# Two attention blocks in one kernel: block B's output projection taken out of block A's attention loop, mask building moved ahead, score matmuls kept in fours

## The chip, the cores and the metric

The kernel runs on one core of a Trainium2 chip. The core has a matmul engine (TensorE, PE in the profile), three engines for elementwise work (VectorE or DVE, ScalarE or ACT, GpSimd or POOL), and DMA queues (here issued from SP and ACT). Matmuls write to PSUM, an accumulator memory of eight banks of 512 float32 values for each of 128 partitions; everything else lies in SBUF. The metric is the device time of one execution in microseconds (us), the median of several executions.

The kernel is written in Tile: the source gives operations on tiles, and a scheduler decides the order of instructions on each engine and adds the waits between them. A tile pool with `bufs=n` holds n tiles in rotation; a tile is given again once all that read it have finished. So the order in which TensorE runs its matmuls is not simply that of the source.

## The reference

Two independent blocks, A and B, each with x of 2048 x 640, 32 heads of 20, in bfloat16. A is attention in a sliding window of 256 positions, B is linear attention. The outputs are set side by side.

```python
def _A_ref(x, wqkv, wo):
    H = 32; Dh = D // H; W = 256
    q, k, v = ...                       # x @ wqkv, split into heads
    scores = jnp.einsum("bhqd,bhkd->bhqk", q, k) * (Dh ** -0.5)
    mask = (idx[:, None] - idx[None, :] >= 0) & (idx[:, None] - idx[None, :] < W)
    p = softmax(jnp.where(mask, scores, -1e9))
    o = jnp.einsum("bhqk,bhkd->bhqd", p, v)
    return o.transpose(...).reshape(B, S, D) @ wo

def _B_ref(x, wqkv, wo):
    q, k, v = ...
    phi = lambda t: jnp.where(t > 0, t + 1, jnp.exp(t)) + 1e-6
    pq, pk = phi(q), phi(k)
    kv = jnp.einsum("bhsd,bhse->bhde", pk, v)
    z = jnp.einsum("bhsd->bhd", pk)
    num = jnp.einsum("bhqd,bhde->bhqe", pq, kv)
    den = jnp.einsum("bhqd,bhd->bhq", pq, z)[..., None] + 1e-6
    return (num / den).transpose(...).reshape(B, S, D) @ wo

return jnp.concatenate([a, b], axis=-1)
```

## The kernel before

Names: P = 128, S = 2048, D = 640, KC = D/P = 5, NB = S/P = 16 token blocks, H = 32, Dh = 20, E21 = 21 (a head's 20 values and a column of ones, whose product is the softmax's or B's denominator).

The kernel transposes both inputs on TensorE (`tps`, line 100), projects keys and values of B and gathers B's 20 x 20 states in `KVacc` (`pb`, lines 136, 161 and 176), projects A's values and A's queries and keys (`aps`, lines 204 and 226), and then B's queries, with phi applied while they leave PSUM:

```python
for ch in range(KC):
    for j0 in range(0, len(tchunks), 2):        # 10 PSUM tiles of two chunks
        ...                                     # 10 matmuls of 512 columns, line 244
        for k, (ts0, tn) in enumerate(sub):
            nc.scalar.activation(out=eqc[:, 0:tn], in_=qps[:, k, 0:tn], func=ACTF.Exp)      # line 252
            nc.vector.tensor_scalar(out=pq_v, in0=qps[:, k, 0:tn], ..., op0=ALU.max, op1=ALU.add)   # 254
            nc.vector.scalar_tensor_tensor(out=pq_v, in0=eqc[:, 0:tn], ..., in1=pq_v, ...)          # 258
```

Then comes A's attention, in eight groups of four heads. `qkg` holds the queries and keys of a group, a head in each quarter of the partitions, copied by DMA from `qkT_u`. For each block j of 128 keys, four score matmuls (one for each head, in its own row group of TensorE) make scores of up to 384 queries, ScalarE takes the exponentials two heads at a time, GpSimd masks the two blocks at the window's edges, and the value matmuls (`do_pv`) of block j - 1 follow. `psST` has three tiles of two PSUM banks, `psB` and `psO` have a bank each:

```python
psB = ctx.enter_context(tc.tile_pool(name="psB", bufs=1, space=bass.MemoryType.PSUM))
psO = ctx.enter_context(tc.tile_pool(name="psO", bufs=1, space=bass.MemoryType.PSUM))
# ... pools, cut
opsring = psO.tile([P, 4, 4 * E21], F32)
for g in range(NG):
    qkg = awork.tile([P, 2, S], BF16)
        # ... DMA into qkg, cut (line 297)
    def do_pv(i):
        ops = opsring[:, i % 4, :]
        kbs = [kb for kb in range(i - 2, i + 1) if kb >= 0]
        for s in range(4):
            h = 4 * g + s
            for ii, kb in enumerate(kbs):
                part = i - kb
                nc.tensor.matmul(
                    ops[:, s * E21:(s + 1) * E21],
                    lhsT=e_tiles[kb][:, s, part * P:(part + 1) * P],
                    rhs=V_aug[:, kb, h * E21:(h + 1) * E21],
                    start=(ii == 0), stop=(ii == len(kbs) - 1),
                )
        ops3 = ops.rearrange("p (s e) -> p s e", e=E21)
        rden = smallp.tile([P, 4, 1], F32, name="rden")
        nc.vector.reciprocal(out=rden[:], in_=ops3[:, :, Dh:E21])
        nc.vector.tensor_tensor(
            out=O_all[:, i, 80 * g:80 * (g + 1)].rearrange("p (s d) -> p s d", d=Dh),
            in0=ops3[:, :, 0:Dh],
            in1=rden.to_broadcast([P, 4, Dh]),
            op=ALU.mult,
        )
        # ... cut
    for j in range(NB):
        nqb = min(3, NB - j)
        nq = nqb * P
        e_t = epool.tile([P, 4, 3 * P], BF16)
        sts = [psST.tile([P, 2, 512], F32, name="st"), psST.tile([P, 2, 512], F32, name="st")]
        for s in range(4):
            nc.tensor.matmul(
                sts[s // 2][:, s % 2, 0:nq],
                lhsT=qkg[32 * s:32 * s + Dh, 1, j * P:(j + 1) * P],
                rhs=qkg[32 * s:32 * s + Dh, 0, j * P:j * P + nq],
                start=True, stop=True,
                tile_position=(32 * s, 0),
            )
        for pair in range(2):
            nc.scalar.activation(
                out=e_t[:, 2 * pair:2 * pair + 2, 0:nq], in_=sts[pair][:, :, 0:nq],
                func=ACTF.Exp, scale=scale,
            )
        nc.gpsimd.affine_select(
            out=e_t[:, :, 0:P], in_=e_t[:, :, 0:P],
            pattern=[[0, 4], [1, P]], compare_op=ALU.is_ge, fill=0.0,
            base=0, channel_multiplier=-1,
        )
        if nqb == 3:
            nc.gpsimd.affine_select(
                out=e_t[:, :, 2 * P:3 * P], in_=e_t[:, :, 2 * P:3 * P],
                pattern=[[0, 4], [-1, P]], compare_op=ALU.is_gt, fill=0.0,
                base=0, channel_multiplier=1,
            )
        e_tiles[j] = e_t
        if j >= 1:
            do_pv(j - 1)
    do_pv(NB - 1)
```

After it in the source, but spread over the attention by the scheduler, which has no dependence to keep it back, comes the rest of block B: a mask built by GpSimd, B's states spread out with it (`KVbd`), and for each token block the numerators, the division, a transpose and the output projection with `Wo_B`, all through the single bank of `psB`:

```python
nc.gpsimd.memset(kvmask[:], 0.0)
for ch, (h0, h1) in enumerate(chunk_heads):
    for h in range(h0, h1 + 1):
        rlo = max(0, Dh * h - ch * P)
        rhi = min(P, Dh * (h + 1) - ch * P)
        c0 = kvoff[ch] + E21 * (h - h0)
        strip = kvmask[:, c0:c0 + E21]
        nc.gpsimd.memset(strip, 1.0)
        nc.gpsimd.affine_select(
            out=strip, in_=strip, pattern=[[0, E21]], compare_op=ALU.is_ge,
            fill=0.0, base=-rlo, channel_multiplier=1,
        )
        nc.gpsimd.affine_select(
            out=strip, in_=strip, pattern=[[0, E21]], compare_op=ALU.is_ge,
            fill=0.0, base=rhi - 1, channel_multiplier=-1,
        )
nc.gpsimd.memset(KVbd[:], 0.0)
# ... KVbd = KVacc * kvmask, six products on VectorE, line 390, cut
for tb in range(NB):
    ...                                          # o_sb = numerators / denominators, lines 427 to 440
    tpsb_t = psB.tile([P, 512], F32, name="pb")
    tpsb = tpsb_t[:].bitcast(BF16).rearrange("p (c t) -> p c t", t=P)
    for c in range(KC):
        nc.tensor.transpose(tpsb[:, c, :], o_sb[:, c * P:(c + 1) * P], ident[:])
    oTb = bw2.tile([P, KC, P], BF16)
    nc.vector.tensor_copy(out=oTb[:], in_=tpsb[:, 0:KC, :])
    osbB = bw2.tile([P, D], BF16)
    for (lo, hi) in [(0, 512), (512, 640)]:
        opt = psB.tile([P, 512], F32, name="pb")
        for c in range(KC):
            nc.tensor.matmul(
                opt[:, 0:hi - lo],
                lhsT=oTb[:, c, :], rhs=Wo_B[:, c, lo:hi],
                start=(c == 0), stop=(c == KC - 1),
            )
        nc.vector.tensor_copy(out=osbB[:, lo:hi], in_=opt[:, 0:hi - lo])
    nc.sync.dma_start(out2[tb * P:(tb + 1) * P, D:2 * D], osbB[:])
```

Last, with the score tiles' banks free, A's output projection:

```python
psAO = ctx.enter_context(tc.tile_pool(name="psAO", bufs=6, space=bass.MemoryType.PSUM, side="right"))
for tb in range(NB):
    tpsA_t = psAO.tile([P, 512], F32, name="pao")
    tpsA = tpsA_t[:].bitcast(BF16).rearrange("p (c t) -> p c t", t=P)
    for c in range(KC):
        nc.tensor.transpose(tpsA[:, c, :], O_all[:, tb, c * P:(c + 1) * P], ident[:])
    oT = awork.tile([P, KC, P], BF16)
    nc.vector.tensor_copy(out=oT[:], in_=tpsA[:, 0:KC, :])
    opa = psAO.tile([P, 512], F32, name="pao")
    opb = psAO.tile([P, 512], F32, name="pao")
    for (tgt, lo, hi) in [(opa, 0, 512), (opb, 512, 640)]:
        for c in range(KC):
            nc.tensor.matmul(
                tgt[:, 0:hi - lo],
                lhsT=oT[:, c, :], rhs=Wo_A[:, c, lo:hi],
                start=(c == 0), stop=(c == KC - 1),
            )
    osb = awork.tile([P, D], BF16)
    nc.scalar.copy(out=osb[:, 0:512], in_=opa[:, 0:512])
    nc.scalar.copy(out=osb[:, 512:640], in_=opb[:, 0:128])
    nc.sync.dma_start(out2[tb * P:(tb + 1) * P, 0:D], osb[:])
```

Of the kernel before, what the change touches and what calls it, by code (L numbers as in the profile page):

```python
# [8 lines left out]
F32 = mybir.dt.float32  # L9
BF16 = mybir.dt.bfloat16  # L10
ALU = mybir.AluOpType
# [4 lines left out]
def kernel(  # L16
# [10 lines left out]
    nc = tc.nc  # L27
# [97 lines left out]

    bc1 = ctx.enter_context(tc.tile_pool(name="bc1", bufs=1))
    KVacc = bc1.tile([P, KVW], F32)
    nc.vector.memset(KVacc[:], 0.0)
    pqT_all = bc1.tile([P, KC, S], BF16)
    psB1 = tc.alloc_tile_pool(name="psB1", bufs=3, space=bass.MemoryType.PSUM)  # L130
# [131 lines left out]
    aload.close()  # L262
    bw1.release()
    xtbp.release()
    psB1.release()
    psB = ctx.enter_context(tc.tile_pool(name="psB", bufs=1, space=bass.MemoryType.PSUM))
    psO = ctx.enter_context(tc.tile_pool(name="psO", bufs=1, space=bass.MemoryType.PSUM))

    oall = ctx.enter_context(tc.tile_pool(name="oall", bufs=1))
    O_all = oall.tile([P, NB, D], BF16)  # L270
    bc2 = ctx.enter_context(tc.tile_pool(name="bc2", bufs=1))
    kvmask = bc2.tile([P, KVW], BF16)
    KVbd = bc2.tile([P, KC, NKV], BF16)
    bw2 = ctx.enter_context(tc.tile_pool(name="bw2", bufs=2))
    NG = H // 4
    awork = ctx.enter_context(tc.tile_pool(name="awork", bufs=2))
    epool = ctx.enter_context(tc.tile_pool(name="epool", bufs=6))
    smallp = ctx.enter_context(tc.tile_pool(name="smallp", bufs=3))
    lctx = ctx.enter_context(ExitStack())
    psST = lctx.enter_context(tc.tile_pool(name="psST", bufs=3, space=bass.MemoryType.PSUM, side="right"))  # L280

    def repack_segments(col):
        c0, p0 = col // P, col % P
        n1 = min(Dh, P - p0)
        segs = [(c0, p0, n1, 0)]
        if n1 < Dh:
            segs.append((c0 + 1, 0, Dh - n1, n1))
        return segs

    opsring = psO.tile([P, 4, 4 * E21], F32)  # L290
    for g in range(NG):
        qkg = awork.tile([P, 2, S], BF16)
        for t in range(2):
            for s in range(4):
                h = 4 * g + s
                for (c0, p0, n, doff) in repack_segments(t * D + h * Dh):
                    nc.sync.dma_start(
                        qkg[32 * s + doff:32 * s + doff + n, t, :],
                        qkT_u[p0:p0 + n, c0, :],
                    )  # L300

        e_tiles = {}

        def do_pv(i):
            ops = opsring[:, i % 4, :]
            kbs = [kb for kb in range(i - 2, i + 1) if kb >= 0]
            for s in range(4):
                h = 4 * g + s
                for ii, kb in enumerate(kbs):
                    part = i - kb  # L310
                    nc.tensor.matmul(  # L311
                        ops[:, s * E21:(s + 1) * E21],
                        lhsT=e_tiles[kb][:, s, part * P:(part + 1) * P],
                        rhs=V_aug[:, kb, h * E21:(h + 1) * E21],
                        start=(ii == 0), stop=(ii == len(kbs) - 1),
                    )
            ops3 = ops.rearrange("p (s e) -> p s e", e=E21)
            rden = smallp.tile([P, 4, 1], F32, name="rden")
            nc.vector.reciprocal(out=rden[:], in_=ops3[:, :, Dh:E21])  # L319
            nc.vector.tensor_tensor(  # L320
                out=O_all[:, i, 80 * g:80 * (g + 1)].rearrange("p (s d) -> p s d", d=Dh),
                in0=ops3[:, :, 0:Dh],
                in1=rden.to_broadcast([P, 4, Dh]),
                op=ALU.mult,
            )
            if i - 2 in e_tiles:
                del e_tiles[i - 2]

        for j in range(NB):
            nqb = min(3, NB - j)  # L330
            nq = nqb * P
            e_t = epool.tile([P, 4, 3 * P], BF16)
            sts = [psST.tile([P, 2, 512], F32, name="st"), psST.tile([P, 2, 512], F32, name="st")]
            for s in range(4):
                nc.tensor.matmul(  # L335
                    sts[s // 2][:, s % 2, 0:nq],
                    lhsT=qkg[32 * s:32 * s + Dh, 1, j * P:(j + 1) * P],
                    rhs=qkg[32 * s:32 * s + Dh, 0, j * P:j * P + nq],
                    start=True, stop=True,
                    tile_position=(32 * s, 0),  # L340
                )
            for pair in range(2):
                nc.scalar.activation(  # L343
                    out=e_t[:, 2 * pair:2 * pair + 2, 0:nq], in_=sts[pair][:, :, 0:nq],
                    func=ACTF.Exp, scale=scale,
                )
            nc.gpsimd.affine_select(  # L347
                out=e_t[:, :, 0:P], in_=e_t[:, :, 0:P],
                pattern=[[0, 4], [1, P]], compare_op=ALU.is_ge, fill=0.0,
                base=0, channel_multiplier=-1,  # L350
            )
            if nqb == 3:
                nc.gpsimd.affine_select(  # L353
                    out=e_t[:, :, 2 * P:3 * P], in_=e_t[:, :, 2 * P:3 * P],
                    pattern=[[0, 4], [-1, P]], compare_op=ALU.is_gt, fill=0.0,
                    base=0, channel_multiplier=1,
                )
            e_tiles[j] = e_t
            if j >= 1:
                do_pv(j - 1)  # L360
        do_pv(NB - 1)

# [33 lines left out]

    num_plan = []
# [20 lines left out]
    for tb in range(NB):  # L418
        den = bw2.tile([P, H, 1], F32)
        o_sb = bw2.tile([P, D], BF16)  # L420
        o_v = o_sb.rearrange("p (h d) -> p h d", d=Dh)
        for bank, (hlo, hhi) in enumerate([(0, 24), (24, 32)]):
            nt = psB.tile([P, 512], F32, name="pb")
            for idx, (ch, bk, c0, ncol) in enumerate(num_plan):
                if bk != bank:
                    continue
                nc.tensor.matmul(  # L427
                    nt[:, c0:c0 + ncol],
                    lhsT=pqT_all[:, ch, tb * P:(tb + 1) * P],
                    rhs=KVbd[:, ch, 512 * bank + c0:512 * bank + c0 + ncol],  # L430
                    start=(idx == first_of_bank[bank]), stop=(idx == last_of_bank[bank]),
                )
            nh = hhi - hlo
# [12 lines left out]
        tpsb_t = psB.tile([P, 512], F32, name="pb")  # L446
        tpsb = tpsb_t[:].bitcast(BF16).rearrange("p (c t) -> p c t", t=P)
        for c in range(KC):
            nc.tensor.transpose(tpsb[:, c, :], o_sb[:, c * P:(c + 1) * P], ident[:])  # L449
        oTb = bw2.tile([P, KC, P], BF16)  # L450
        nc.vector.tensor_copy(out=oTb[:], in_=tpsb[:, 0:KC, :])
        osbB = bw2.tile([P, D], BF16)
        for (lo, hi) in [(0, 512), (512, 640)]:
            opt = psB.tile([P, 512], F32, name="pb")
            for c in range(KC):
                nc.tensor.matmul(  # L456
                    opt[:, 0:hi - lo],
                    lhsT=oTb[:, c, :], rhs=Wo_B[:, c, lo:hi],
                    start=(c == 0), stop=(c == KC - 1),
                )  # L460
            nc.vector.tensor_copy(out=osbB[:, lo:hi], in_=opt[:, 0:hi - lo])  # L461
        nc.sync.dma_start(out2[tb * P:(tb + 1) * P, D:2 * D], osbB[:])

    lctx.close()
    psAO = ctx.enter_context(tc.tile_pool(name="psAO", bufs=6, space=bass.MemoryType.PSUM, side="right"))
    for tb in range(NB):
        tpsA_t = psAO.tile([P, 512], F32, name="pao")
        tpsA = tpsA_t[:].bitcast(BF16).rearrange("p (c t) -> p c t", t=P)
        for c in range(KC):
            nc.tensor.transpose(tpsA[:, c, :], O_all[:, tb, c * P:(c + 1) * P], ident[:])  # L470
        oT = awork.tile([P, KC, P], BF16)
        nc.vector.tensor_copy(out=oT[:], in_=tpsA[:, 0:KC, :])  # L472
        opa = psAO.tile([P, 512], F32, name="pao")
        opb = psAO.tile([P, 512], F32, name="pao")
        for (tgt, lo, hi) in [(opa, 0, 512), (opb, 512, 640)]:
            for c in range(KC):
                nc.tensor.matmul(  # L477
                    tgt[:, 0:hi - lo],
                    lhsT=oT[:, c, :], rhs=Wo_A[:, c, lo:hi],
                    start=(c == 0), stop=(c == KC - 1),  # L480
                )
        osb = awork.tile([P, D], BF16)
        nc.scalar.copy(out=osb[:, 0:512], in_=opa[:, 0:512])
# [32 lines left out]
```

The softmax here doesn't subtract the row's maximum and nothing guards it: scores larger than these inputs give would overflow.

## Time and profile before

| | |
|---|---|
| median time | 486.66 us (485.58 to 555.08) |
| span of the profiled execution | 553.2 us |
| PE busy | 512.8 us, 3612 matmuls |
| ACT busy | 242.7 us |
| DVE busy | 236.1 us |
| POOL busy | 173.5 us |

The profiled execution took longer than the others, at a TensorE clock below full speed that differs between the stages, so times of TensorE read from it must be scaled before they are set against the median.

How to read the views: a busy line gives, for each engine, the time in which it had an instruction of the program running, with the number of instructions; PEclk is the clock that TensorE was granted, as a share of full speed. The chain of work is followed back from the last instruction to what released it. In a list of waits, `X <- Y: a, b, c` means that X stood idle for a us in b waits, the longest of c us, each ended by Y. A line in order of time starts with its start and duration in us.

### The profile page before, as it was taken

To read this page: it belongs to the slowest core of one execution; us is meant where nothing else is said; L and a number is where in the kernel's file an instruction comes from. 1 tells how busy PE (TensorE), PEld (TensorE's weight loads), DVE (VectorE), ACT (ScalarE), POOL (GpSimd) and SP (SyncE) were. 2 spreads that over 40 slices of the span, in tenths; PEclk is the share of its full clock that TensorE was granted. 3 is DMA by queue.
4 is the path that set the end of the run, shared out by engine and by line. 5 is a ranking of instruction groups with operands and counts; after the bars stand their busy time and mean duration, and the time that the engine had idled before them with its cause. 6 is when DMAs were issued, how large, how long until landed. Compare 5 with 4: busy or idle time off the path is not lost.

```text
span 553.2 us, 9204 instructions
## 1 busy us (share of the span) xinstructions
PE 512.8 (93%) x3612; PEld 255.8 (46%) x3612; DVE 236.1 (43%) x651; ACT 242.7 (44%) x377; POOL 173.5 (31%) x373
## 2 busy tenths in 40 slices
PE   3399999999999998879999999999999999998786
PEld 2276655555533333334444445454444544444443
DVE  2176666666521224884334344334444444431111
ACT  0011111111211122337777777778777777771222
POOL 0010000000000009306565655566565665650000
PEclk9966666666666666665555555555555555555666
DMA  8940000000000004000020111202020200001111
GB/s 308 375 171 2 0 1 1 0 2 0 2 0 0 1 0 95 1 0 13 13 62 2 43 31 27 48 14 61 1 60 13 55 20 14 13 13 37 47 60 47
DMA packets 14154, 22.86 MB, mean 41 GB/s; under 512 B 1440, under 2 KB 11552, under 8 KB 14112
## 3 DMA queue, kind: packets, MB, share of 16 engines
q1 hardware_dynamic: 10688, 17.21, 10.6%
q10 hardware_dynamic: 3424, 5.08, 2.6%
q8 instruction: 28, 0.46, 0.4%
q14 instruction: 14, 0.11, 0.1%
HBM read 11.80 MB, written 5.24 MB: 31 GB/s over the span
## 4 chain that ended last, share of the span: by engine, by line
PE 84%; DMA 4%; DVE 4%; POOL 4%; SPq 1%; issue 1%; ACT 1%; ACTq 0%; DVEq 0%; POOLq 0%
PE st L335 20%; PE aps L226 12%; PE pb L456 9%; PE opsring L311 9%; PE pao L477 6%; PE pb L161 6%; PE pb L136 6%; PE aps L204 5%; DMA Wb<-in_B_wqkv_dram 4%; PE pb L427 3%; PE aps L244 3%; PE pb L449 2%; POOL kvmask L371 1%; PE pb L176 1%; DVE oT L472 1%; PE pao L470 1%
## 5 line engine op out<-in xcount | busy, mean ns | idle before, releaser
L343 ACT ACTIVATE e_t<-st 128x768 bf16<-128x768 f32 (+2 forms) x256 | 187.4, 773 | 63.9 <-PE st L335 44.0
L335 PE MATMUL st<-qkg 20*128 20x384 bf16 (+2 forms) x512 | 137.0, 476 | 3.4 <-issue 2.9
L347 POOL TENSOR_SCALAR_AFFINE_SELECT e_t<-e_t 128x512 bf16<-128x512 bf16 x128 | 81.3, 635 | 125.5 <-ACT e_t L343 125.3
L311 PEld LDWEIGHTS <-e_t 128*128 128x128 bf16 x1440 | 65.0, 109 | 58.4 <-issue 56.5
L311 PE MATMUL opsring<-V_aug,e_t 128*128 128x21 bf16 x1440 | 76.7, 184 | 1.1 <-DVE O_all L320 1.1
L353 POOL TENSOR_SCALAR_AFFINE_SELECT e_t<-e_t 128x512 bf16<-128x512 bf16 x112 | 71.1, 635 | 0.0
L226 PE MATMUL aps<-xT_A,Wqk_u 128*128 128x512 bf16 x200 | 68.0, 512 | 0.0
L319 DVE RECIPROCAL rden<-opsring 128x4 f32<-128x4 f32 x128 | 23.2, 181 | 98.7 <-PE opsring L311 97.9
L456 PE MATMUL pb<-Wo_B,oTb 128*128 128x512 bf16 (+1 forms) x160 | 56.0, 459 | 0.6 <-DVE osbB L461 0.2
L204 PE MATMUL aps<-Wv_A,xT_A 128*128 128x480 bf16 (+1 forms) x160 | 42.2, 392 | 9.3 <-DMA Wv_A<-in_A_wqkv_dram 8.9
L477 PE MATMUL pao<-Wo_A,oT 128*128 128x512 bf16 (+1 forms) x160 | 35.3, 388 | 9.0 <-DVE oT L472 9.0
L335 PEld LDWEIGHTS <-qkg 20*128 20x128 bf16 x512 | 29.0, 99 | 29.1 <-issue 19.8
L226 PEld LDWEIGHTS <-Wqk_u 128*128 128x128 bf16 x200 | 23.9, 120 | 37.0 <-issue 36.6
L136 PE MATMUL pb<-Wb,xT_B 128*128 128x320 bf16 x160 | 37.5, 391 | 0.0
L236 ACT CAST qkT_u<-aps 128x512 bf16<-128x512 f32 x20 | 11.7, 586 | 58.0 <-DVE qkT_u L234 58.0
L147 ACT ACTIVATE ek<-pb 128x320 bf16<-128x320 f32 x32 | 14.0, 437 | 52.5 <-PE pb L136 52.5
L157 POOL MEMSET V<- 128x32 bf16 x16 | 3.7, 244 | 103.2 <-PE pb L176 103.2
L244 PE MATMUL aps<-xT_B,Wb 128*128 128x512 bf16 x100 | 34.1, 519 | 2.1 <-DVE pqT_all L254 2.0
L161 PE MATMUL pb<-Wb,xT_B 128*128 128x480 bf16 (+1 forms) x160 | 35.7, 390 | 0.0
L320 DVE TENSOR_TENSOR O_all<-opsring,rden 128x80 bf16<-128x80 f32 x128 | 30.8, 241 | 4.2
L234 DVE CAST qkT_u<-aps 128x512 bf16<-128x512 f32 x20 | 13.8, 690 | 42.5 <-PE aps L226 42.5
L477 PEld LDWEIGHTS <-oT 128*128 128x128 bf16 x160 | 15.2, 114 | 29.0 <-issue 15.8
(52 smaller groups left out, 442.0 us busy)
## 6 DMA issues: line engine op xcount, KB each, us to landing
qkg<-qkT_u SPq DMA_DIRECT2D x56, 80.0 KB
x_nat_A<-in_A_x_dram SPq DMA_DIRECT2D x4, 640.0 KB
x_nat_B<-in_B_x_dram ACTq DMA_DIRECT2D x4, 640.0 KB
out_dram<-osbB SPq DMA_DIRECT2D x16, 160.0 KB
out_dram<-osb SPq DMA_DIRECT2D x16, 160.0 KB
Wb<-in_B_wqkv_dram SPq DMA_DIRECT2D x1, 2400.0 KB
Wqk_u<-in_A_wqkv_dram ACTq DMA_DIRECT2D x1, 1600.0 KB
Wv_A<-in_A_wqkv_dram SPq DMA_DIRECT2D x1, 800.0 KB
```

The source lines that it names most:

```text
L136: nc.tensor.matmul(pb[:, 0:hi - lo], lhsT=xT_B[:, kc, tb * P:(tb + 1) * P], rhs=Wb[:, kc, D + lo:D + hi], start=(kc == 0), stop=(kc == KC ...
L161: nc.tensor.matmul(pb[:, 0:hi - lo], lhsT=xT_B[:, kc, tb * P:(tb + 1) * P], rhs=Wb[:, kc, 2 * D + lo:2 * D + hi], start=(kc == 0), stop=(k ...
L204: nc.tensor.matmul(vps[:, bank, 0:hi - lo], lhsT=xT_A[:, kc, kb * P:(kb + 1) * P], rhs=Wv_A[:, kc, lo:hi], start=(kc == 0), stop=(kc == KC ...
L226: nc.tensor.matmul(qps[:, k, 0:tn], lhsT=Wqk_u[:, kc, c * P:(c + 1) * P], rhs=xT_A[:, kc, ts0:ts0 + tn], start=(kc == 0), stop=(kc == KC - 1),
L244: nc.tensor.matmul(qps[:, k, 0:tn], lhsT=Wb[:, kc, ch * P:(ch + 1) * P], rhs=xT_B[:, kc, ts0:ts0 + tn], start=(kc == 0), stop=(kc == KC - 1),)
L311: nc.tensor.matmul(ops[:, s * E21:(s + 1) * E21], lhsT=e_tiles[kb][:, s, part * P:(part + 1) * P], rhs=V_aug[:, kb, h * E21:(h + 1) * E21] ...
L335: nc.tensor.matmul(sts[s // 2][:, s % 2, 0:nq], lhsT=qkg[32 * s:32 * s + Dh, 1, j * P:(j + 1) * P], rhs=qkg[32 * s:32 * s + Dh, 0, j * P:j ...
L343: nc.scalar.activation(out=e_t[:, 2 * pair:2 * pair + 2, 0:nq], in_=sts[pair][:, :, 0:nq], func=ACTF.Exp, scale=scale,)
L347: nc.gpsimd.affine_select(out=e_t[:, :, 0:P], in_=e_t[:, :, 0:P], pattern=[[0, 4], [1, P]], compare_op=ALU.is_ge, fill=0.0, base=0, channe ...
L353: nc.gpsimd.affine_select(out=e_t[:, :, 2 * P:3 * P], in_=e_t[:, :, 2 * P:3 * P], pattern=[[0, 4], [-1, P]], compare_op=ALU.is_gt, fill=0. ...
L456: nc.tensor.matmul(opt[:, 0:hi - lo], lhsT=oTb[:, c, :], rhs=Wo_B[:, c, lo:hi], start=(c == 0), stop=(c == KC - 1),)
L477: nc.tensor.matmul(tgt[:, 0:hi - lo], lhsT=oT[:, c, :], rhs=Wo_A[:, c, lo:hi], start=(c == 0), stop=(c == KC - 1),)
```

## The change

It does five things:

- The mask and `KVbd` are built ahead: `kvmask` and `KVacc` move to a pool that exists from the beginning, `KVbd` to one that is there before the projections, and the code that fills them stands before the attention.
- Of block B only the numerators and the division stay in the attention: `numer` is called for one token block after score blocks 5 and 12 of each group, tied behind the last score matmul by a manual dependence (an order on TensorE, no wait for another engine). Its result stays in SBUF, in `O_all_B`.
- The value matmuls come two score blocks late and not one, and the first of them is tied behind the fourth score matmul of the block, so that all four score matmuls are issued first.
- B's transposes and its output projection move to the end, to those of A. The last stage has 32 halves (16 token blocks, A and B), and the transposes of the next half are issued ahead of the matmuls of this one.
- Pools: `epool` has 5 tiles and not 6, `awork` is opened with `reuse_waits="tile"`, and the last stage has tiles of its own.

It is meant to take out of the attention what can run elsewhere, and to keep the score matmuls of a block together.

```diff
+    KVacc = xtbp.tile([P, KVW], F32)
+    nc.vector.memset(KVacc[:], 0.0)
+    kvmask = xtbp.tile([P, KVW], BF16)
     bc1 = ctx.enter_context(tc.tile_pool(name="bc1", bufs=1))
-    KVacc = bc1.tile([P, KVW], F32)
-    nc.vector.memset(KVacc[:], 0.0)
     pqT_all = bc1.tile([P, KC, S], BF16)
+    KVbd = bc1.tile([P, KC, NKV], BF16)
 ... (kvmask and KVbd filled before the attention's pools are opened, code unchanged)
-    awork = ctx.enter_context(tc.tile_pool(name="awork", bufs=2))
-    epool = ctx.enter_context(tc.tile_pool(name="epool", bufs=6))
+    oball = ctx.enter_context(tc.tile_pool(name="oball", bufs=1))
+    O_all_B = oball.tile([P, NB, D], BF16)
+    awork = ctx.enter_context(tc.tile_pool(name="awork", bufs=2, reuse_waits="tile"))
+    epool = ctx.enter_context(tc.tile_pool(name="epool", bufs=5))
 ...
-    for tb in range(NB):
+    def numer(tb, after):
         den = bw2.tile([P, H, 1], F32)
-        o_sb = bw2.tile([P, D], BF16)
-        o_v = o_sb.rearrange("p (h d) -> p h d", d=Dh)
+        o_v = O_all_B[:, tb, :].rearrange("p (h d) -> p h d", d=Dh)
 ... (numerators and division as before, and:)
+                if idx == first_of_bank[bank]:
+                    tc.add_manual_dep(
+                        mm.ins, after.ins.name,
+                        mybir.DependencyInfo(mybir.DependencyClass.NoSync, mybir.DependencyReason.DATA),
+                        reason="spread numerators",
+                    )
-        tpsb_t = psB.tile([P, 512], F32, name="pb")
 ... (the rest of B's loop: transposes, copy, output projection, copies, store, removed)
-        def do_pv(i):
+        def do_pv(i, after=None):
 ...
+                    if after is not None and s == 0 and ii == 0:
+                        tc.add_manual_dep(
+                            mm.ins, after.ins.name, ...
+                            reason="whole pair first",
+                        )
 ...
-            if j >= 1:
-                do_pv(j - 1)
+            if j >= 2:
+                do_pv(j - 2, pair_end)        # pair_end: the block's fourth score matmul
+            if j in (5, 12):
+                numer(2 * g + (j == 12), last_st)
+        do_pv(NB - 2)
         do_pv(NB - 1)
 ...
-    for tb in range(NB):                      # A's output projection, as above
+    tailw = ctx.enter_context(tc.tile_pool(name="tailw", bufs=2))
+    psAO = ctx.enter_context(tc.tile_pool(name="psAO", bufs=6, space=bass.MemoryType.PSUM, side="right"))
+    halves = [(tb, s) for tb in range(NB) for s in (0, 1)]
+
+    def head(tb, s):
+        src = O_all if s == 0 else O_all_B
+        tps_t = psAO.tile([P, 512], F32, name="pao")
+        tpsv = tps_t[:].bitcast(BF16).rearrange("p (c t) -> p c t", t=P)
+        for c in range(KC):
+            nc.tensor.transpose(tpsv[:, c, :], src[:, tb, c * P:(c + 1) * P], ident[:])
+        oTx = tailw.tile([P, KC, P], BF16, name="oTx", bufs=3)
+        nc.vector.tensor_copy(out=oTx[:], in_=tpsv[:, 0:KC, :])
+        return oTx
+
+    nxt = head(*halves[0])
+    for n, (tb, s) in enumerate(halves):
+        oTx = nxt
+        if n + 1 < len(halves):
+            nxt = head(*halves[n + 1])
+        Wo = Wo_A if s == 0 else Wo_B
 ... (matmuls into oa and ob, 512 and 128 columns)
+        ox = tailw.tile([P, D], BF16, name="ox", bufs=4)
+        nc.scalar.copy(out=ox[:, 0:512], in_=oa[:, 0:512])
+        nc.scalar.copy(out=ox[:, 512:640], in_=ob[:, 0:128])
+        nc.sync.dma_start(out2[tb * P:(tb + 1) * P, s * D:(s + 1) * D], ox[:])
```

## The prediction

> **What bounds the kernel now.** I read the profile in this order: busy time by stage, the chain of work through one stage, the waits, and the time order of single engines. The stages follow from the chain: projections up to 205.80, the query projection of block B to 248.40, attention to 498.00, the output projection of A to the end.
>
> ```profile
> core 0: us, PE busy (x) PEld busy (x) DVE busy (x) ACT busy (x) POOL busy (x), PEclk, DMA share, GB/s
> 38.90:153.50 114.60, 114.60 (x602) 65.09 (x600) 70.96 (x138) 19.34 (x49) 3.35 (x14) 0.65 0.00 1
> 153.50:205.80 52.30, 52.30 (x161) 19.31 (x160) 11.50 (x18) 9.37 (x16) 0.00 (x0) 0.65 0.00 0
> 205.80:248.40 42.60, 35.51 (x120) 13.26 (x119) 29.14 (x53) 12.55 (x22) 20.01 (x110) 0.64 0.15 31
> 248.40:498.00 249.60, 247.07 (x2317) 120.09 (x2316) 101.42 (x390) 187.37 (x256) 146.29 (x239) 0.50 0.11 28
> 498.00:553.20 55.20, 42.99 (x264) 22.44 (x261) 8.63 (x20) 12.06 (x32) 0.64 (x1) 0.64 0.13 48
> ```
>
> Attention is nearly half of the span. TensorE is busy in all of it, but at clock 0.50, while the other stages have 0.64 or 0.65; ScalarE is busy 187.37 of 249.60. Eight head groups share it, so a group takes 31.2 us, with 23.4 us of ScalarE. The chain through one group (436.4 to 467.5) shows how TensorE spends it:
>
> ```profile
> by line: PE st L335 46.8%; PE pb L456 20.6%; PE opsring L311 19.9%; PE pb L427 7.0%; PE pb L449 3.8%; DVE osbB L461 2.3%; issue 0.3%
> ...
> 455.45 0.43 PE st L335
> 455.88 0.37 PE opsring L311 x10
> 456.25 0.43 PE st L335 x2
> 456.68 0.97 PE pb L456 x2
> 457.65 0.05 PE opsring L311 x2
> 457.70 0.43 PE st L335 x2
> ```
>
> One score matmul and two of them cost the same 0.43 us: matmuls of different row groups run together. In the program's order the 512 score matmuls fall into 272 runs, 150 of two and 94 of one; as fours they would be 128. So the st share, 46.8% of 31.1 = 14.5 us, is some 34 runs of 0.43, where 16 steps could do with 16. ScalarE waits for it, and when fed it follows on faster than its mean of 0.813 us:
>
> ```profile
> ACT e_t L343 <- PE st L335: 44.0, 81, 1.7
> ```
>
> ```profile
> 420.90 3.11 ACT L343 ACTIVATE e_t<-st 128x768 bf16<-128x768 f32 x4 [0.46 <-PE st L335]
> 427.19 1.54 ACT L343 ACTIVATE e_t<-st 128x768 bf16<-128x768 f32 x2 [0.71 <-PE st L335]
> ```
>
> The second of two adds 1.54 - 0.81 = 0.73 us. Two further stages matter. In the query projection the chain runs over the mask building on GpSimd, 206.14 to 226.30 us, because VectorE's queue holds the masked products between evictions:
>
> ```profile
> 226.09 0.21 POOL kvmask L375
> 226.30 0.02 issue
> 226.33 0.31 DVE KVbd L390
> 226.64 0.60 DVE pqT_all L258
> ```
>
> And in the last stage each token block takes 3.16 us, of which TensorE waits for a copy:
>
> ```profile
> 516.10 2.17 PE pao L477 x10
> 518.27 0.43 PE pao L470 x5
> 518.69 0.02 issue
> 518.72 0.50 DVE oT L472
> 519.22 0.05 issue
> ```
>
> **What the Trainium skill says.** "TensorE: Matmul & The Clock Gate", Part 1: The HAM clock gate, has two states, half rate when the array is little busy and full rate after some 3.4 us of dense work. The trace agrees on the half (0.50 in attention), but not on gaps as the only cause: attention has no TensorE gap of that length. Its 0.65 is not one of the two states, so I take it as a full rate that was cut in the profiled execution. The same page, Part 3: Packing small matmuls, says that a weight load overlaps matmuls in flight only where the row groups differ. The trace agrees: 384 columns at half of 2.4 GHz (that page's clock) would be 0.32 us, and a run of scores before full-height work costs 0.43. "Trainium Kernel Development and Optimization", Performance Expectations, warns that matmul busy time is a bad metric; here 247.07 of 249.60 busy would hide that half of the score time is bad order.
>
> **Scaling to the metric.** The metric is 486.66, the profiled span 553.2, so 66 us have to be placed. With full clock where 0.65 was granted, and 0.50 unchanged in attention: the stage to 153.50 repeats a 6.59 us token block of TensorE alone; at full clock that is 4.3, but VectorE is busy 4.18 of it with waits between, so I take 5.0: 16 x 1.6 = 26 saved. To 205.80: 52.3 x 0.35 = 18. To 248.40: GpSimd's 20 us stay, then 11 of the 20 chunks at 2 x 0.685 = 1.37 of VectorE, 35.5 in all: 7. Last stage: (2.17 + 0.43) x 0.65 + 0.57 = 2.26 for 3.16: 16 x 0.9 = 14. Sum 65, so 488: it fits. The other reading, attention alone faster, needs 249.6 to fall to 183, below the 249.6 x 0.50 / 0.65 = 192 of pure clock and below ScalarE's 187: unlikely, but it is the first rival.
>
> **The change part by part**, on the timed scale.
>
> 1. *Until 205.80.* The order is the same but for a few transposes. GpSimd builds the mask at the start, where it has nothing else to do; the six masked products (1.7 us) go between evictions of a stage in which VectorE is busy 11.50 of 52.30. Time: 205.8 - 26 - 18 = 161.
>
> 2. *Query projection of B.* No mask, and its 100 matmuls stand in one run. TensorE needs 100 x 0.325 x 0.65 = 21, VectorE 20 x 1.37 = 27. So 28 instead of 35.5.
>
> 3. *Attention.* From a group's chain go L456 (20.6% of 31.1 = 6.4), L449 (1.2) and the osbB wait (0.7): 8.3 us, 66 over all groups. The score matmuls become fours: the built order has 142 runs, 108 of four, each followed by 12 opsring matmuls. The fourth still needs a PSUM pair that the exponentials free, so I count up to two waves of 0.32 a step and 0.11 for the change: 16 x 0.75 = 12.0 for 14.5. With opsring 6.2 and numerators 2.2, TensorE has 20.4 us a group. ScalarE has at least 28 x 0.73 + 2 x 0.51 + 2 x 0.33 = 22.1 (the shorter ones as spacing in the trace), and by its busy time 23.4. GpSimd's masks are 30 x 0.59 = 18. ScalarE becomes the bound: 23.4 x 8 = 187, and 1 for the start: 188 instead of 249.6.
>
> 4. *Tail.* Sixteen B halves are added and each copy moves beside the matmuls before it: the next half's five transposes are issued ahead. A half costs (2.17 + 0.43) x 0.65 = 1.69 of TensorE; ScalarE's copies are 0.59 + 0.27, VectorE's 0.49. So 32 x 1.69 = 54, 3 to 4 until the clock rises (it did 3 us into the old tail), and 3 for the last copy and store: 61 instead of 41.
>
> Sum: 161 + 28 + 188 + 61 = **438 us**, a ratio of 0.90. In short: attention gives 62, the mask 7.5, the tail takes back 20.
>
> **The rivals.**
>
> *The attention of the timed runs was already faster.* Then it was at ScalarE's bound before, nothing is gained there, and the tail at clock 0.65 pays in full: 205.8 + 34 + 188 + 32 x 2.6 + 8 = 519. For it: the clock of a timed run isn't shown. Against it: the sum above.
>
> *Lockstep.* Six PSUM banks hold three score pairs, two to a step. Each four needs a pair that the last exponentials just freed, and TensorE (20.4), GpSimd (18) and ScalarE (22 to 23) all have about the same work. If each step loses 0.2 us in handing over, a group is 26.6 and the sum 464. For it: only one bank serves the numerators, and their second part stands inside a four. Against it: the value matmuls now come two steps late, so masks have a whole step, and a pair is written about 0.7 us before it is read.
>
> *A slow tail.* At clock 0.50 a half costs 3.4 and the tail 54 more: 492, no gain. Against it: the old tail, with a gap of 0.57 in each 3.16, was granted the higher clock.
>
> **Range and chances.** [...] the range reaches further up: attention 170 (ScalarE's best spacing) to 210, the rest within 8: 418 to 460. The first and third rivals have 5% each, and a mixture of them might land near the old time. Faster by over 2%: 0.90; within 2%: 0.04; slower: 0.06.
>
> **What would show it.** In the changed profile: no kvmask in the chain after the projections, and a query stage near 28 to 33; eight groups of about 23.5 us with ScalarE busy over 90% and its wait for st well under 44 us; st runs of four on TensorE; a tail without the oT wait, at the higher clock, of 32 equal halves of 1.7 us (2.6 if the clock is cut). It is wrong if ScalarE's wait for st stays, if GpSimd's masks or the numerators' bank release the value matmuls late, or if the tail runs at 0.50.

## The result and the profile after

The changed kernel takes 418.23 us (417.54 to 418.97), beside 486.37 for the kernel before: a ratio of 0.860, 95% interval 0.859 to 0.861. The prediction was 438, range 418 to 460.

Busy time by stage of the changed kernel, in the columns known from before: start; projections (two rows); query projection of B; attention; tail.

```profile
core 0: us, PE busy (x) PEld busy (x) DVE busy (x) ACT busy (x) POOL busy (x), PEclk, DMA share, GB/s
0.00:43.70 43.70, 22.93 (x217) 17.26 (x218) 19.55 (x46) 2.65 (x6) 18.56 (x119) 1.00 0.77 271
43.70:115.10 71.40, 70.83 (x524) 44.23 (x523) 61.23 (x120) 18.54 (x45) 5.33 (x15) 1.00 0.00 1
115.10:152.90 37.80, 37.75 (x183) 17.31 (x181) 15.43 (x29) 9.80 (x17) 0.00 (x0) 1.00 0.00 1
152.90:182.20 29.30, 23.06 (x102) 9.68 (x101) 26.29 (x41) 12.53 (x21) 0.00 (x0) 1.00 0.22 45
182.20:358.20 176.00, 166.36 (x2088) 83.81 (x2089) 81.58 (x348) 171.68 (x256) 144.93 (x239) 0.50 0.11 24
358.20:417.30 59.10, 55.57 (x504) 35.49 (x503) 16.68 (x38) 24.14 (x65) 0.99 (x2) 0.95 0.26 90
```

The clock is now 1.00 in the dense stages and still 0.50 in attention, which is how the timed runs were read in the prediction. ScalarE is busy 171.68 of 176.00 in attention. Its waits there, and its order of time in one group:

```profile
ACT e_t L442 <- POOL e_t L446: 2.9, 7, 0.4
ACT e_t L442 <- DVE pqT_all L260: 1.6, 1, 1.6
ACT e_t L442 <- PE st L432: 0.6, 1, 0.6
```

```profile
280.47 9.25 ACT L442 ACTIVATE e_t<-st 128x768 bf16<-128x768 f32 x13
```

The wait for scores fell from 44.0 us to 0.6. Thirteen exponentials in a row take 9.25 us: (9.25 - 0.81) / 12 = 0.70 each. The chain through attention alone would not name ScalarE as the bound, since it changes engines at every short wait and gives TensorE more than ScalarE:

```profile
by line: ACT e_t L442 30.2%; PE st L432 21.5%; PE opsring L402 13.3%; issue 12.7%; PE pb L354 8.0%; DVE O_all_B L373 4.5%; DVE den L372 2.4%; DVE O_all L417 2.0%; DVE den L367 1.7%; DVE rden L416 1.5%; POOL e_t L446 1.0%; POOL e_t L452 0.7%
```

Which engine it is has to be shown by giving each of them more work (e6 and e7 below).

GpSimd builds the mask in the first row (18.56 us busy), and the chain through the query projection holds VectorE and no GpSimd:

```profile
by line: DVE pqT_all L260 47.1%; DVE pqT_all L256 42.9%; PE aps L246 7.4%; ACT eqc L254 2.1%; issue 1.7%; PE aps L228 0.7%
```

In the tail the chain is TensorE alone until the last half's copy and store, one half every 1.64 us, and the wait for the copy is gone:

```profile
389.88 1.36 PE pao L490 x10
391.24 0.28 PE pao L475 x5
391.51 1.36 PE pao L490 x10
```

### The profile page after: what moved, and what is told of

It is laid out like the page before. It is cut to its first block, busy times and chain, and to the rows that moved or that the text cites. A ratio compares the mean times of both kernels' runs of the same rounds, so it can differ in the third digit from the quotient of the medians.

```text
span 417.3 us, 9224 instructions
## 1 busy us (share of the span) xinstructions
PE 376.5 (90%) x3612; PEld 207.8 (50%) x3612; DVE 220.8 (53%) x619; ACT 239.3 (57%) x409; POOL 169.8 (41%) x373
## 4 chain that ended last, share of the span: by engine, by line
PE 57%; ACT 14%; DVE 14%; DMA 7%; issue 6%; POOL 1%; SPq 0%; ACTq 0%; DVEq 0%; POOLq 0%
ACT e_t L442 13%; PE pao L490 11%; PE aps L228 10%; PE st L432 9%; PE opsring L402 6%; PE pb L138 5%; DMA Wo_A<-in_A_wo_dram 4%; PE aps L206 4%; PE pb L163 4%; PE pb L354 3%; DMA x_nat_A<-in_A_x_dram 3%; DVE pqT_all L260 3%; DVE pqT_all L256 3%; PE pao L475 2%; PE pb L178 2%
## 5 line engine op out<-in xcount | busy, mean ns | idle before, releaser
L442 ACT ACTIVATE e_t<-st 128x768 bf16<-128x768 f32 (+2 forms) x256 | 171.7, 823 | 5.2 <-POOL e_t L446 2.9
L432 PE MATMUL st<-qkg 20*128 20x384 bf16 (+2 forms) x512 | 108.9, 469 | 10.0 <-ACT e_t L442 4.6
L402 PEld LDWEIGHTS <-e_t 128*128 128x128 bf16 x1440 | 50.2, 105 | 41.2 <-issue 38.2
L402 PE MATMUL opsring<-V_aug,e_t 128*128 128x21 bf16 x1440 | 61.1, 182 | 1.9 <-POOL e_t L446 0.4
L228 PE MATMUL aps<-xT_A,Wqk_u 128*128 128x512 bf16 x200 | 45.6, 379 | 0.0
L496 ACT CAST ox<-pao 128x512 bf16<-128x512 f32 x32 | 18.7, 585 | 32.1 <-ACT ox L497 23.3
L490 PEld LDWEIGHTS <-oTx 128*128 128x128 bf16 x320 | 26.4, 100 | 19.7 <-issue 1.6
L477 DVE COPY oTx<-pao 128x640 bf16<-128x640 bf16 x32 | 15.7, 491 | 35.8 <-PE pao L475 35.8
L138 PE MATMUL pb<-Wb,xT_B 128*128 128x320 bf16 x160 | 26.2, 299 | 0.0
L490 PE MATMUL pao<-Wo_A,oTx 128*128 128x512 bf16 (+1 forms) x160 | 25.6, 310 | 0.0
```

The lines of the kernel that those rows point to most:

```text
L138: nc.tensor.matmul(pb[:, 0:hi - lo], lhsT=xT_B[:, kc, tb * P:(tb + 1) * P], rhs=Wb[:, kc, D + lo:D + hi], start=(kc == 0), stop=(kc == KC ...
L228: nc.tensor.matmul(qps[:, k, 0:tn], lhsT=Wqk_u[:, kc, c * P:(c + 1) * P], rhs=xT_A[:, kc, ts0:ts0 + tn], start=(kc == 0), stop=(kc == KC - 1),
L402: mm = nc.tensor.matmul(ops[:, s * E21:(s + 1) * E21], lhsT=e_tiles[kb][:, s, part * P:(part + 1) * P], rhs=V_aug[:, kb, h * E21:(h + 1) * ...
L432: last_st = nc.tensor.matmul(sts[s // 2][:, s % 2, 0:nq], lhsT=qkg[32 * s:32 * s + Dh, 1, j * P:(j + 1) * P], rhs=qkg[32 * s:32 * s + Dh, ...
L442: nc.scalar.activation(out=e_t[:, 2 * pair:2 * pair + 2, 0:nq], in_=sts[pair][:, :, 0:nq], func=ACTF.Exp, scale=scale,)
L490: nc.tensor.matmul(tgt[:, 0:hi - lo], lhsT=oTx[:, c, :], rhs=Wo[:, c, lo:hi], start=(c == 0), stop=(c == KC - 1),)
```

## The experiments

My theory: attention was set by TensorE at half clock; moving block B's projection away and keeping the scores together each shorten TensorE's part until ScalarE sets it, near 22 us a group. Rivals: the scores' order alone does it; TensorE or the hand-over through PSUM is the bound still; the clock would follow TensorE's load. "Attention" below is the time from the first exponential to the end of the last, 249.6 us in the profile before and 175.3 in the changed kernel.

### The mask alone, and all but the mask

```diff
  e1: the kernel before
+     kvmask, KVacc from xtbp; KVbd from bc1; filled before the attention's pools are opened
  e2: the changed kernel
-     kvmask, KVacc from xtbp; KVbd from bc1
+     KVacc from bc1; kvmask, KVbd from a pool opened after the projections
```

> The kernel before with the mask and KVbd built ahead, and nothing else of the change. Theory (the mask held up VectorE's evictions in the query projection of B, and nothing hides that): 7 us less than before, about 479. Rival (the stall is made good later, since TensorE has other work): 485 to 486.

> The changed kernel with the mask built where it was before, after the projections. Theory: 418 + 7 = 425, all of it in the query projection of B. Rival (in the changed kernel the masked products are in nobody's way): 418 to 420.

Measured: 478.36 us for 486.07 before in the first, 7.7 less; 425.79 in the second, 7.6 more than the changed kernel. So the part is worth the same alone and with the rest. The first run also shows the old attention and the old tail at the clock of the timed runs:

```profile
183.40:432.90 249.50, 242.99 (x2298) 119.88 (x2312) 101.31 (x390) 187.34 (x256) 146.25 (x239) 0.50 0.11 28
432.90:477.00 44.10, 31.20 (x260) 18.39 (x263) 8.62 (x20) 12.11 (x33) 0.64 (x1) 0.93 0.16 60
```

Attention is again 249.5 us at 0.50. That settles the first rival of the prediction: this execution took 477.0 us, as long as the timed runs of its kernel, and the old attention in it was not faster.

### The order of the score matmuls

```diff
  e3: the changed kernel
-            if j >= 2:
-                do_pv(j - 2, pair_end)
+            if j >= 1:
+                do_pv(j - 1)
-        do_pv(NB - 2)
  e9: the changed kernel
-                do_pv(j - 2, pair_end)
+                do_pv(j - 2)
```

> The changed kernel with the value matmuls one score block late and untied, as before; block B's projection stays in the tail. TensorE's order then has 220 runs of score matmuls instead of 142. Theory (ScalarE is the bound at 22 us a group, and the move of B's projection alone brings TensorE down to about that): 220/8 = 27.5 runs of 0.43 plus 6.2 and 2.2 make TensorE 20 to 23 us a group, so 5 to 12 us more, 423 to 430. Rival (the fours are the main gain): the runs cost all of 78 x 0.43 = 34 us, 450 or more.

> The changed kernel with the value matmuls still two score blocks late, but not tied behind the fourth score matmul. TensorE's order then has 242 runs of score matmuls, 212 of them of two. Theory (TensorE's time in a group goes with its runs: 220 runs gave 23.8 us a group): 30 runs a group, 24 to 25 us, 18 to 25 us more than the changed kernel, 436 to 443. Rival (being two blocks late is what helped, by giving the masks time): within 5 us of the changed kernel.

Measured: 433.86 and 441.64 us, 15.6 and 23.4 more than the changed kernel; attention 191.7 and 199.5 (23.8 and 24.9 us a group, for 21.8). The second came as expected: two blocks late without the tie is worse than neither, so what helps is the order that the tie makes. The first cost more than the 5 to 12 us expected. A group's chain, by line and for a stretch of it, shows why:

```profile
by line: PE st L432 35.2%; PE opsring L402 29.7%; DVE O_all L417 8.5%; PE pb L354 8.2%; DVE rden L416 6.5%; issue 3.8%; ACT e_t L442 3.4%; POOL e_t L446 2.7%; DVE O_all_B L373 1.4%; DVE den L372 0.9%; DVE den L367 0.7%; POOLq L446 0.1%
```

```profile
268.28 0.25 DVE O_all L417
268.57 0.20 PE opsring L402 x2
268.78 0.43 PE st L432
269.20 0.39 PE opsring L402 x10
269.83 0.25 DVE O_all L417
270.12 0.20 PE opsring L402 x2
```

One block takes 1.55 us here, and VectorE stands in the chain: all four slots of `opsring` lie in one PSUM bank, and the first value matmuls of a block wait until VectorE has read the block before. O_all and rden, VectorE's two reads, have 8.5% and 6.5% of the chain; GpSimd's masks, which the value matmuls follow more closely here, have 2.7%. No run gave the slots banks of their own, so this part is read from the chain and not shown by an experiment. I had counted TensorE's runs alone. The tie alone, with value matmuls one block late, wasn't run: the scheduler's order on TensorE is then the same as that of the first edit. So the fours need both, the delay and the tie.

### Block B's projection back in the attention

```diff
  e4: the changed kernel, in numer()
+        # transposes of O_all_B[:, tb] into psB, copy, 10 matmuls with Wo_B, copies, store: as before
  and in the tail
-    halves = [(tb, s) for tb in range(NB) for s in (0, 1)]
+    halves = [(tb, s) for tb in range(NB) for s in (0,)]
```

> The changed kernel with block B's transposes and output projection back in the attention, each behind its numerators; the score matmuls stay together (165 runs). Theory: TensorE in a group is about 20 + 7.6 = 27 to 28 us and again the bound, attention about 215 for 176, and the tail is 16 halves shorter, 26 us: 427 to 435. Rival (the fours are the main gain, attention stays near ScalarE's bound): 176 + 0 to 10 in attention and 26 less in the tail, 395 to 402, faster than the changed kernel.

Measured: 433.72 us, attention 216.3, tail 32.8. The times are those of the theory, and the rival, by which this would have been the best version, falls. So the move costs 59.1 - 32.8 = 26.3 us in the tail and saves 216.3 - 175.3 = 41.0 in attention. With the result above:

| version | attention, us |
|---|---|
| before | 249.6 |
| scores together, projection in attention (e4) | 216.3 |
| projection moved, scores apart (e3) | 191.7 |
| both | 175.3 |

The two alone take 33.3 and 57.9 us away. Together that would be 158.4, but attention ends at 175.3. I take the difference, 17 us or 2.1 a group, as slack of TensorE under ScalarE's bound. But this is a sum of unlike parts, for the clock was not 0.50 throughout in e4:

```profile
182.60:398.90 216.30, 199.11 (x2299) 105.70 (x2314) 101.93 (x392) 174.46 (x256) 145.16 (x239) 0.56 0.12 31
```

In each group one stretch of 3.4 us had full clock (281.20 to 284.60, for one). By an estimate from this, such a stretch can do what takes 6.8 us at half clock, so up to 8 x 3.4 = 27 of the 33.3 us may be the clock's and not the order's; how much isn't shown. At 0.50 on both sides the move is worth 57.9 us (before against e3) and then the order 16.4 (e3 against both), 74.3 together. The new pools and the tied numerators are in all versions but the first, and were not run alone.

### Which engine sets the attention now

```diff
  e6: the changed kernel
+            if j in (2, 9):
+                numer(2 * g + (j == 9), last_st)      # each block's numerators a second time
  e7: the changed kernel, with a pool scrp of two tiles
+            scr = scrp.tile([P, 256], BF16)           # read by nobody
+            nc.scalar.activation(out=scr[:], in_=Wo_A[:, 0, 0:256], func=ACTF.Exp, scale=scale)
  e8: the changed kernel
-    psST = ... tc.tile_pool(name="psST", bufs=3, ...)
+    psST = ... tc.tile_pool(name="psST", bufs=2, ...)
```

> The changed kernel with each block's numerators and division done a second time in the attention (after score blocks 2 and 9): about 2.2 us of TensorE and 2.4 us of VectorE more in each group, and no work for ScalarE. Theory (ScalarE is the bound, TensorE has 1 to 2 us of slack a group): 0 to 8 us more, 418 to 426. Rival (TensorE is still the bound): 8 x 2.2 = 18 us more, 436.

> The changed kernel with one more exponential of 128x256 from SBUF into a tile that nobody reads, in each of the 128 score blocks: 0.33 us of ScalarE each, no work for other engines. Theory (ScalarE is the bound of the attention): 128 x 0.33 = 42 us more, 460. Rival (TensorE or GpSimd is): 0 to 15 us more.

> The changed kernel with two score tiles instead of three in PSUM, so that a score block is written only into what the exponentials of the block before have just freed. Theory (the third tile is what keeps hand-overs off ScalarE's path): 0.1 to 0.3 us lost in each of 128 blocks, 13 to 38 us more. Rival (the hand-over hides behind the other tile's exponential): 0 to 5 us more.

More work for TensorE: 419.37 us, 1.1 more, and attention is 0.5 longer. A block's ten numerator matmuls take 0.52 + 0.33 us in the chain of the changed kernel, so some 14 us were added. TensorE's idle time alone wouldn't have told that they fit: it was 176.00 - 166.36 = 9.6 us in the changed kernel, and here it is 4.8:

```profile
183.10:358.90 175.80, 170.97 (x2243) 92.85 (x2243) 108.50 (x443) 171.97 (x256) 145.51 (x239) 0.50 0.11 24
```

So TensorE has slack for 14 us at least, and isn't the bound. More work for ScalarE: 449.16, which is 31 more and not 42. The added ones wait for nothing, and the scheduler put 48 of them ahead of the first exponential of scores, which starts 11.3 us later; the other 80 make the attention 19.8 us longer. In a late group every block has one:

```profile
337.20:363.20 26.00, 21.79 (x266) 10.80 (x265) 10.42 (x44) 26.00 (x50) 18.43 (x30) 0.50 0.12 27
```

ScalarE is busy 26.00 of 26.00, and the group is longer than 21.8 by 4.2, 0.26 for each of 16 blocks, while TensorE has its old work. So nearly all that ScalarE is given, the attention gets longer by. GpSimd, with 18.27 us of work in a group of 21.83, was given no more in any run. With two score tiles instead of three: 445.42, attention 202.1, 0.21 us lost in each of 128 blocks, as the lockstep rival would have it; its wait for scores is back:

```profile
ACT e_t L442 <- PE st L432: 17.6, 25, 1.2
```

So the third tile is what keeps the hand-over off ScalarE's path.

### The transposes ahead in the tail

```diff
  e5: the changed kernel
-    nxt = head(*halves[0])
     for n, (tb, s) in enumerate(halves):
-        oTx = nxt
-        if n + 1 < len(halves):
-            nxt = head(*halves[n + 1])
+        oTx = head(tb, s)
```

> The changed kernel with each half's transposes issued just ahead of its own matmuls in the tail. Theory (the copy from PSUM then stands between them, as in the old tail, 0.5 to 0.6 us a half): 32 x 0.57 = 18 us more, 436. Rival (waits of that kind also lower the granted clock in the tail): 470 or more.

Measured: 442.66 us, 24.4 more, or 0.76 a half, at full clock. TensorE waits for the copy 0.6 us in each half again:

```profile
389.90 1.53 PE L487 MATMUL pao<-Wo_A,oTx 128*128 128x512 bf16 x9 [0.58 <-DVE oTx L477]
```

Without this the tail is 82.7 us, and most of what the move saves in attention (58 us) would go again (82.7 - 44.1 = 39). With it the tail is 59.1 - 44.1 = 15.0 longer than the old one, and the account closes: 7.7 for the mask, 74.3 less in attention and 15.0 more in the tail make 67.0 of the 68.1 us measured.

### The granted clock in attention

```diff
  e10, e11: the changed kernel, in each score block
+            fill = psB.tile([P, 512], F32, name="pb")
+            for rpt in range(1):                      # e11: range(2)
+                nc.tensor.matmul(fill[:], lhsT=pqT_all[:, 0, 0:P], rhs=pqT_all[:, 0, 0:512],
+                                 start=True, stop=True)      # tied behind last_st
```

> The changed kernel with one matmul of 128x512 more in each score block, into the numerators' bank, read by nobody: only work for TensorE. Theory (the attention is granted half the clock whatever it does): 16 x 0.43 = 6.8 us a group more on TensorE, of which 2 to 3 are slack: about 4 us a group, 30 to 40 us in all, 450 to 458. Rival (the clock goes by how much of the time the array really streams columns, and this lifts it): a granted clock above 0.5 in attention and 418 to 425.

> The same with two such matmuls in each score block. Theory of a fixed half clock: 13.7 us a group more, about 11 of them on the path, 88 us in all, 505. Rival (the clock rises with streaming): full clock, 418 to 430, so more work for TensorE would cost less than half of it.

Measured: 450.34 and 467.38 us (the second is the median of 467.27, 467.38 and 470.48; a fourth execution took 476.73); attention 207.1 and 224.4. Busy time in attention, first with one more matmul in each block, then with two:

```profile
182.60:389.70 207.10, 204.27 (x2199) 97.86 (x2199) 80.87 (x346) 176.77 (x256) 145.08 (x239) 0.50 0.10 21
```

```profile
182.40:406.70 224.30, 213.40 (x2331) 103.25 (x2329) 79.84 (x346) 176.33 (x256) 145.05 (x239) 0.75 0.09 19
```

Neither theory holds whole. One matmul more leaves the clock at 0.50 and costs what the half-clock theory said. Two lift it to 0.75 in the mean, in windows of 0.50 and of 1.00 in turn:

```profile
311.20:318.00 6.80, 6.80 (x45) 2.50 (x44) 1.25 (x6) 4.13 (x6) 3.56 (x7) 0.50 0.00 0
318.00:324.80 6.80, 6.17 (x99) 3.65 (x97) 3.77 (x16) 6.80 (x12) 5.73 (x11) 1.00 0.01 2
```

In the window at half clock TensorE is busy all of the time and ScalarE 4.13 us of 6.80; in the one at full clock ScalarE is busy throughout. Later groups take 27.3 us with two, 26.0 with one: the second matmul costs 1.3 us a group, the first 4.2. It buys no time, but it shows that the clock goes by what is on TensorE, not by how long it is busy: with one matmul more it is busy in 204.27 of 207.10 us, at 0.50, with two in 213.40 of 224.30, at 0.75. What exactly is counted stays open.

### A version that beats both

```diff
  e12: the changed kernel, in the query projection of B
-                    nc.vector.tensor_scalar(out=pq_v, in0=qps[:, k, 0:tn], scalar1=0.0, scalar2=1e-6,
-                                            op0=ALU.max, op1=ALU.add)
+                    if k == 0:
+                        nc.vector.tensor_scalar(...)           # as before
+                    else:
+                        nc.scalar.activation(out=pq_v, in_=qps[:, k, 0:tn], func=ACTF.Relu)
```

It leaves out the 1e-6 of phi in half of the queries.

> The changed kernel with one part of the query projection of B moved: in every second chunk ScalarE takes max(x, 0) (without the 1e-6, which is below the rounding of the result), and VectorE only adds. Theory (VectorE's 1.36 us a chunk set that stage, 29.3 us for 21.5 of matmuls): VectorE 20.6, ScalarE 18, so TensorE sets it: 4 to 6 us less, 412 to 414. Rival (the chain through PSUM sets it): 0 to 2 us less.

Measured: 415.15 us, 3.1 less than the changed kernel; ratio to the kernel before 0.855, interval 0.853 to 0.856. The stage fell from 29.3 to 26.1 us and not to the 22 of the matmuls. Its chain now goes from engine to engine:

```profile
by line: DVE pqT_all L263 25.6%; DVE pqT_all L257 23.0%; ACT eqc L254 22.2%; ACT pqT_all L262 18.7%; PE aps L246 5.6%; issue 3.7%; ACT e_t L445 3.0%; ACTq L262 0.1%; ACTq L445 0.1%
```

So VectorE's load was part of the bound; by this chain the rest is the series of reads of one PSUM tile by ScalarE and VectorE in turn, which no run took apart.

## Why the prediction was right

The profiled span after is 417.3 us; by the prediction's own steps:

| step | predicted | measured |
|---|---|---|
| until the end of A's projections | 161 | 152.9 |
| query projection of B, to the first exponential | 28 | 30.0 |
| attention | 188 | 175.3 |
| tail | 61 | 59.1 |
| sum | 438 | 417.3 |

- *Scaling to the metric: right.* Full clock in the dense stages and 0.50 in attention is what the runs show. The size of the first stage was off: I took 5.0 us for a token block because VectorE was busy 4.18 and would wait between. It took 4.65 (16 blocks begin from 43.66 to 113.40): in the chain from 62 to 80 us VectorE has only 16%. That is 5.6 of the 8 us; the others lie before. That the same scaling gave 488 for the old kernel was partly luck: in e1, whose stages but one are the old ones, A's projections end at 153.0 us for 161, but the old query projection (30.4 in e1, and 7.7 for the mask) and the old tail took about 38 and 44.1 for 35.5 and 41.
- *Query projection: right.* VectorE sets it at 1.34 us a chunk (155.91 to 182.82 for 20), for 1.37 worked out; the way in, a first PSUM tile and its exponential, takes 3.0 us, for which the sum had 1. The mask is worth 7.7 us, predicted 7.5.
- *Attention: mechanism right, the term mis-sized.* ScalarE became the bound. I put 23.4 us for a group, its busy time in the old profile, over a floor of 22.1. Both came from a ScalarE that was kept waiting: the profile counts an exponential as 0.81 us, but when fed the next starts 0.70 later, for 0.73 in the two-in-a-row that I took as the best. So a group takes 21.8; 8 x 1.6 = 13 us. The 66 us that leave TensorE's chain were about right as a count (57.9 alone), and the rest of the gain is the order (16.4 as the last part; the 33.3 of e4 has stretches of full clock in it). The 0.11 us that the prediction adds for a change between scores and full-height work is 0.43 less 0.32, an estimate from the clock on the page that it cites. That it is an exposed weight load isn't shown: in the new tail ten loads for full-height matmuls are busy 1.40 us (from 409.31), and the ten matmuls of a half take 1.36 in the chain, so there the loads overlap matmuls of the same rows.
- *Tail: right.* 1.64 us a half for 1.69. The clock rose 5.4 us into the tail, not 3 to 4; in the old profile, too, it was 0.50 until 503.20, 5.2 us into the tail and not the 3 that the prediction read. The copy's part of an old block was 0.57 us, as read, but a whole block took 2.40 in e1 (447.58 to 449.98) for 2.26, so the old tail was 44.1 and not 41.
- *Rivals.* The first is excluded by e1. Lockstep didn't happen, but e8 shows that it would have with one tile less. The slow tail didn't happen.

Three errors of the same sign (8, 13 and 2), less one of 2, made the value 20 us too high. The measured 418.23 lies 0.2 us above the lower edge of the range, and three of the eight executions lie below it: that it fell inside is luck, while the mechanism, ScalarE's bound after TensorE's, is what the runs show. The largest error came from taking a time measured under a wait for the engine's own.

## What to carry to other kernels

Where one engine sets a stage at a lower granted clock than the stages beside it, work moved out of that stage costs less where it lands (here 26.3 us for 41.0), if what would wait there is issued ahead. Two ways of relieving one engine don't add up once another becomes the bound: work out that engine's floor from the spacing of its instructions when they are fed, not from its busy time. Matmuls of different row groups should stand together in the order on TensorE, and a delay in the source alone doesn't make the scheduler do it.

## What the runs showed of the hardware

- TensorE was granted 0.50 in attention, but for at most its first 1.1 us, in twelve of the fourteen kernels, while it was busy 87 to 99% of the time. In the other two, dense 128x512 matmuls between the small ones came with stretches of full clock (3.4 us in each group of e4, 6.8 us in the one shown of e11; means of 0.56 and 0.75); the old kernel and e10 have such matmuls too, at 0.50. The Trainium skill ("TensorE: Matmul & The Clock Gate", Part 1: The HAM clock gate) gives idle time as what halves the clock. In e2 that is seen: TensorE stood idle for 3.91 and 3.86 us while the mask was built, and the clock was 0.50 from 167.10 to 173.90. In attention it was halved without, with no gap of TensorE over 1.1 us, so idle time is not the only cause, and the measurement decides.
- A 128x768 exponential from PSUM takes 0.81 us by its own duration and 0.70 in a fed queue.
- Value matmuls into one PSUM bank waited for VectorE's reads of other columns of that bank, because the program orders the two; these reads made up 15% of a group's chain in e3.
